# Threshold attention and a squared-ReLU network on one core: one order of steps for all periods, a weight chunk converted every second period

## The chip, the core and the metric

The kernel runs on one core of a Trainium2 chip. The metric is the device time of one launch, in microseconds, as the median of three runs. Five engines work side by side, each through its own queue in order, and wait for each other by semaphores: TensorE (PE; PEld is its weight load), VectorE (DVE), ScalarE (ACT), GpSimd (POOL) and SyncE (SP), which here issues nearly all DMAs.

## What is computed

```python
# q, k, v: (8, 8, 576, 64) float32; tau = 0.02
scores = (1 / 8) * q @ k.transpose(0, 1, 3, 2)
thresh = max(scores, axis=-1) - tau
scores = where(scores >= thresh, scores, -1e9) - max(scores)
attn = exp(scores); attn = attn / (attn.sum(-1) + 1e-9)
x = (attn @ v), heads side by side          # (4608, 512)
h = maximum(x @ w_in, 0)                    # w_in (512, 2048)
out = h * h @ w_out                         # w_out (2048, 512)
```

The two weight matrices come as 64-bit floats and are turned into 32-bit ones on the chip, by integer operations on their two halves.

## The kernel before

**Two stages.** The first is the attention, the second the network in fast-multiplication form (products of sums of blocks, seven instead of eight, twice nested). While the attention runs, the weights are fetched, converted and summed for the second stage. Nothing of the network's products starts before the attention's last products, since both need the same PSUM banks.

**Units and periods.** A unit is 128 query rows with two heads side by side. There are 144 units, two to a period (A and B), so 72 periods. For each unit the kernel makes these steps:

- `SA`, `RA`, `SB`, `RB`: scores by TensorE into six PSUM banks (L459), 512 keys and the last 64.
- `top` (L477, VectorE, two a unit): copies scores to SBUF and takes the row maximum on the way (the scores are negated, so it is a minimum). These are the maximum passes. `least` (L484, GpSimd, one a unit, 128x2) adds tau.
- `pow` (L487, ScalarE, two a unit): the exponential. `mask` (L492, VectorE, two a unit): zeroes what is under the threshold and sums. `over` and `inv` (L499 GpSimd, L502 VectorE): the reciprocal of the sums.
- `V`, `W`, `U` (L403, TensorE): turn the weights by transposes, `V` and `U` into the one pair of banks `pt`, `W` into banks 2 and 3. `Q` (L542) spreads the reciprocals beside `W`. `eV`, `eU`, `eW` (L552, ScalarE) copy them out. `T` and `eT` turn queries and keys of a later pair of heads (L423, L428, L436) in eight periods of nine.
- `PV` (L561, TensorE): the weights times the values, into the first columns of banks 0 and 5. `x` (L708 ScalarE, L710 VectorE) copies the two halves out, `xm` (L720, GpSimd) multiplies with the reciprocal, and the result goes to DRAM.

**Conversion.** A chunk of weights is 128x512 and takes six steps: `c1` (L209, ScalarE), `c2` (L216) and `c3` (L223) on GpSimd, `c4` (L231) and `c5` (L239) on VectorE, `c6` (L249) on GpSimd. There are 32 chunks. They are begun in periods 2 to 33, one in each (L592), and end one period later. Raw chunks lie in seven buffers in the part of the weight store that the block sums with outer index 5 and 3 fill later (L142, L189).

**Block sums.** 44 additions of 128x512 by GpSimd (L123, L126, made by `sums`, L261) turn the converted blocks into the operands of the network. They run after the conversion, at the steps `s1` and `s2`, and then the first operand of the network (`prepare_x`, L860) is made in the same places.

**The order.** No scheduler decides: the program's order on each engine is the order of the words in a list, one list for a period with conversion (`CONVERTING`, periods 2 to 34), one for a period without (`PLAIN`). A minus sign after a word means the step of the period before, two mean two before. Two first periods and the last ones have lists of their own. `step` (L763) makes a step once, after the same step of the earlier period. PSUM dependences between engines go by whole banks (`touch`, L378): whoever writes a bank waits for the last reader on each other engine, and a reader waits for the other engines' last access too.

The difference between the two lists that matters most is the second half of `x`: while weights are converted, ScalarE copies both halves and GpSimd scales both (L720, 128x256). Without conversion VectorE takes the second half out of PSUM and scales it at once (L710), and GpSimd scales one (128x128).

Of the kernel before, what the change touches and what calls it, by code (L numbers as in the profile page):

```python
# [48 lines left out]
def kernel(  # L49
# [54 lines left out]
    sb, cv = Region(arena, 0, X_AT[0]), Region(arena, X_AT[0], ARENA)  # L104
# [37 lines left out]
    raw_places = Region(wall, OUTER.index(5) * 7 * BANK, 49 * BANK)  # L142
# [61 lines left out]
    def convert1(m):  # L204
        if m not in raws:
            return
        lo, hi = pick(raws[m], 0), pick(raws[m], 1)
        a = cv.tile([P, WC], I32, tag="a", bufs=6, name="a")
        nc.scalar.activation(out=a.bitcast(FP32), in_=hi.bitcast(FP32), func=AF.Abs)  # L209
        parts[m] = (lo, hi, a)  # L210
        raws.pop(m)
# [49 lines left out]
    def sums(W, which, at):  # L261

        first = [at[a][b] for a in range(2) for b in range(2)]

        def inner(m, kinds):
            for op, o, x, y in kinds:
                to = W[m, o] if o == y else weight_tile(W, m, o)
                yield op(nc.gpsimd, to[:, :], W[m, x][:, :], W[m, y][:, :])

        early = which[0:3]  # L270
        for m in (1, 2):
            yield from inner(m, early)
        for op, o, x, y in which:
            for k_ in first:
                to = W[o, k_] if o == y else weight_tile(W, o, k_)
                yield op(nc.gpsimd, to[:, :], W[x, k_][:, :], W[y, k_][:, :])
        for m in OUTER:
            yield from inner(m, which[3:] if m in (1, 2) else which)
# [185 lines left out]
    def softmax(n):  # L464
# [39 lines left out]
        soft[n] = dict(top=top, least=least, power=power, mask=mask, over=over, inverse=inverse)  # L504
# [49 lines left out]
    def values(m):  # L554

        for c in range(CH):
# [35 lines left out]
    starts = {m + 2: m for m in range(16 + EARLY)}  # L592
    X_FIRST = 40
    summing = deque([sums(W_IN, SUMS_A, AT_A)])

    def sums_due(p):

        return p > max(starts) + 2 and not converts(p)

    def sums_step():  # L600
        while summing and next(summing[0], 0) == 0:
            summing.popleft()
# [10 lines left out]
    def converts(p):  # L613
        return is_wide and (has_chunk(p) or has_chunk(p - 1))

# [3 lines left out]
    def begun(n):  # L619
# [12 lines left out]
    """.split()  # L632
# [3 lines left out]
        fetch SA RA RB SB topA0 T topA1 leastA topB0 topB1 leastB powA0 powA1 eT more powB0 powB1 maskA0  # L636
        maskA1 maskB0 maskB1
        """.split(),
        1: """
        fetch ahead SA RA RB SB T eT more over topA0 topA1 leastA inv V topB0 topB1 leastB powA0 powA1 eV W  # L640
        Q powB0 eW maskA0 maskA1 powB1 maskB0 maskB1
# [3 lines left out]
    BEGIN_WITH[NU // 2 + 1] = """  # L645
        give eU-- powA0-- V-- powA1-- eV-- maskA1-- PV-- powB1-- powB0-- maskA0-- U- W-- Q-- x--
        maskB1-- maskB0-- eW-- over- inv- eU- xm-- PV- x- V- eV- W- Q- eW- xm- U eU PV x xm
        """.split()

    def spots():  # L650
        return [(sc[:, ds(b * BANK + REST, (FULL + 1) * HALF)], b * BANK) for b in (1, 4)]

# [8 lines left out]
    def period(p):  # L661

        A, B_, a, b = 2 * p, 2 * p + 1, 2 * p - 2, 2 * p - 1
        m, turns = p - 2, TURNS.get(p, ())
# [16 lines left out]
        def W():  # L681
            if has(2 * m + 2):
                pt["W"] = two_banks(w_bank(m + 1))
                fill(m + 1, "W", pt["W"], w_bank(m + 1) * BANK)

        def Q():
            if has(2 * m + 2):
                spread_sums(m + 1, pt["W"], w_bank(m + 1) * BANK)
# [8 lines left out]
        def PV():  # L697
            if has(2 * m):
                values(m)

        def values_out():
            if not has(2 * m):
                return
            late["x"] = x = sb.tile([P, 2, P], FP32, tag="x", bufs=3, name="x")
            for j in range(2):
                from_ = sc[:, ds(5 * j * BANK, P)]
                if converts(p) or j == 0:
                    made = nc.scalar.copy(x[:, j, :], from_)  # L708
                else:
                    made = nc.vector.tensor_tensor(  # L710
                        out=x[:, j, :], in0=from_, in1=wT[m][:, ts(SCALE_AT + j, P)], op=ALU.mult
                    )
                touch("x", made, 5 * j * BANK, P, m)

        def given_out():
            if has(2 * m):
                x = late.pop("x")
                made = x[:, 0 : 1 + converts(p), :].rearrange("p j n -> p (j n)")
                scale = wT[m][:, ds(SCALE_AT * P, (1 + converts(p)) * P)]
                nc.gpsimd.tensor_tensor(out=made, in0=made, in1=scale, op=ALU.mult)  # L720
                wT.pop(m)
                valued(m)
                give_x(m, x)

# [9 lines left out]
        def every(key):  # L734
# [4 lines left out]
            "U": lambda: fills("U", m), "V": lambda: fills("V", m + 1), "W": W, "Q": Q, "T": turn_some,  # L739
            "eU": lambda: evict("U", m), "eV": lambda: evict("V", m + 1), "eW": lambda: evict("W", m + 1),  # L740
            "eT": lambda: every("turn"),
            "SA": lambda: scored(A), "SB": lambda: scored(B_),
            "RA": lambda: scored_rest(A), "RB": lambda: scored_rest(B_),
            "PV": PV, "x": values_out, "xm": given_out,
            "c1": lambda: convert1(begun(p)), "c2": lambda: convert2(begun(p)),
            "c3": lambda: convert3(begun(p)), "c4": lambda: convert4(begun(p - 1)),
            "c5": lambda: convert5(begun(p - 1)), "c6": lambda: convert6(begun(p - 1)),
            "s1": lambda: sums_due(p) and sums_step(), "s2": lambda: sums_due(p) and p < 60 and sums_step(), "ahead": lambda: ahead(5), "more": lambda: ahead(7),
            "fetch": lambda: (fetch(begun(p + 2)), fetch(begun(p + 3)) if p > 1 else None), "put": put, "give": lambda: ask(False),
        }  # L750
        steps["over"] = lambda: do(a, "over")
        steps["inv"] = lambda: do(a, "inverse")
        for letter, n in (("A", A), ("B", B_)):
            for what, name in (("least", "least"),):
                steps[what + letter] = lambda n=n, name=name: do(n, name)
            for what, name in (("top", "top"), ("pow", "power"), ("mask", "mask")):
# [3 lines left out]

    tables, made_steps = {}, set()

    def step(name, p):  # L763
# [3 lines left out]
        step(name, p - 1)  # L767
        made_steps.add((name, p))
# [4 lines left out]
    def run_period(p):  # L773

        for name in BEGIN_WITH.get(p) or (CONVERTING if converts(p) else PLAIN):
# [404 lines left out]
    with tc.manual_schedule():  # L1180
        with ExitStack() as stack:
# [25 lines left out]
            for p in range(FIRST_PERIOD, NU // 2 + 6):  # L1207
# [5 lines left out]
                if p == X_FIRST + 4:  # L1213
                    summing.append(prepare_x(0, lambda op, out, x, y: op(nc.gpsimd, out, x, y)))
            for _ in range(60):
                sums_step()
# [201 lines left out]
```

## Time and profile before

| what | value |
|---|---|
| time, median of 3 runs | 1272.29 us (1269.83 to 1273.04) |
| profiled execution: its span, first to last instruction | 1273.4 us |
| what lies around the span | not shown; the span stands 1.1 us above the median of the runs |
| attention, from the first row of the trace to the network's first product | 494.8 us |
| network | 778.6 us |
| busy share of the span: PE, DVE, ACT, POOL | 98%, 78%, 66%, 77% |

The page gives the busy time of each engine over the whole span. The two stages have different limits, so the page's shares say little about the attention: its stretches have to be asked for by themselves. A view by windows gives each engine's busy time in a stretch, a timeline gives start and length of each instruction. In a full queue the distance from one start to the next is what an instruction costs; its length overlaps the next one a little (a maximum pass is 0.75 us long and the next begins 0.68 us after it).

### The profile page before, as it was taken

The numbers are of one execution on the slowest core, as the hardware profiler recorded it, in microseconds if no ns is written. First come the engines' busy times: TensorE is split into PE (matmuls) and PEld (weight loads), VectorE is DVE, ScalarE is ACT, GpSimd is POOL, SyncE is SP. The second block draws the span as 40 slices with busy tenths as digits, with TensorE's granted clock in tenths as the row PEclk, the third lists the DMA queues.
The fourth block names the chain that finished last, engine by engine and source line by source line (L and its number), as shares of the span: only waits on it lengthen the run. The fifth ranks groups of instructions, "written<-read, shape, count | busy, mean of one in ns | idle before, by whom it ended". The sixth has DMA issues, their size and how long they took to land.

```text
span 1273.4 us, 55161 instructions
## 1 busy us (share of the span) xinstructions
PE 1251.7 (98%) x22991; PEld 1093.6 (86%) x22991; DVE 988.2 (78%) x2385; ACT 844.3 (66%) x1536; POOL 982.5 (77%) x1070
## 2 busy tenths in 40 slices
PE   8999999999999999999999999999999999999998
PEld 5777776777777778988888888999999999999998
DVE  6999998999999996886887878867746654665463
ACT  6999998999999994666765856675524432443240
POOL 2999998877776542988898989868787878787776
PEclk8999999999999999999999999999999999999999
DMA  7566677434333323657667657579965336533511
GB/s 186 143 161 154 167 198 188 120 89 107 89 81 89 83 53 97 192 166 237 202 191 231 215 169 249 172 274 369 267 163 152 83 107 163 146 84 107 167 35 35
DMA packets 289912, 196.79 MB, mean 155 GB/s; under 512 B 98560, under 2 KB 250624, under 8 KB 289664
## 3 DMA queue, kind: packets, MB, share of 16 engines
q1 hardware_dynamic: 288352, 192.86, 52.8%
q8 instruction: 181, 2.97, 1.0%
q14 instruction: 67, 0.55, 0.1%
q10 hardware_dynamic: 1312, 0.41, 0.1%
HBM read 120.85 MB, written 72.35 MB: 152 GB/s over the span
## 4 chain that ended last, share of the span: by engine, by line
PE 72%; DMA 3%; ACT 2%; POOL 2%; DVE 1%; issue 1%; DVEq 0%; ACTq 0%; POOLq 0%; SPq 0%
PE po L818 27%; PE ph L997 17%; PE ph L818 10%; PE sc L561 7%; PE sc L459 6%; PE pt L403 4%; PE sc L542 1%; PE sc L423 1%; POOL arena L126 1%; DMA g<-arena 1%; ACT arena L970 1%; DVE arena L126 1%; DMA w<-arena 1%; ACT arena L971 1%; ACT c L857 1%
## 5 line engine op out<-in xcount | busy, mean ns | idle before, releaser
L126 POOL TENSOR_TENSOR arena<-arena 128x512 f32<-128x512 f32 (+1 forms) x314 | 378.7, 1224 | 125.1 <-DVE arena L126 113.5
L818 PE MATMUL po<-wall,arena 128*64 128x128 f32 x7056 | 385.8, 273 | 1.4 <-ACT arena L813 0.8
L818 PEld LDWEIGHTS po<-wall,arena 128*64 128x64 f32 x7056 | 385.1, 137 | 1.9 <-ACT arena L813 1.0
L126 DVE TENSOR_TENSOR arena<-ph,arena 128x512 f32<-128x512 f32 x378 | 254.5, 688 | 77.4 <-PE ph L997 30.9
L123 POOL TENSOR_TENSOR arena<-arena 128x128 f32<-128x128 f32 (+1 forms) x322 | 265.5, 826 | 24.1 <-DMA arena<-w 8.5
L997 PE MATMUL ph<-arena,wall 128*128 128x256 f32 x1176 | 256.7, 380 | 2.3 <-DVE arena L126 2.1
L997 PEld LDWEIGHTS ph<-arena,wall 128*128 128x128 f32 x1176 | 222.4, 190 | 36.3 <-DVE arena L126 6.2
L126 DVE TENSOR_TENSOR arena<-po,arena 128x128 f32<-128x128 f32 x378 | 107.6, 288 | 159.3 <-PE po L818 151.4
L492 DVE SCALAR_TENSOR_TENSOR arena<-arena 128x576 f32<-128x576 f32 x288 | 225.9, 820 | 0.4 <-ACT arena L487 0.3
L487 ACT ACTIVATE arena<-arena 128x576 f32<-128x576 f32 x288 | 214.1, 781 | 13.4 <-DVE arena L477 13.3
L477 DVE TENSOR_SCALAR_CACHE_REDUCE arena<-sc 128x576 f32<-128x576 f32 x288 | 203.4, 752 | 18.5 <-ACT arena L552 5.7
L857 ACT COPY c<-arena 128x512 f32<-128x512 f32 (+1 forms) x295 | 168.9, 578 | 70.1 <-DVE arena L123 36.1
L459 PE MATMUL sc<-arena 64*64 64x512 f32 (+1 forms) x2304 | 179.6, 415 | 5.6 <-ACT arena L552 1.2
L561 PE MATMUL sc<-arena 64*64 64x128 f32 (+1 forms) x5760 | 165.6, 261 | 1.0 <-ACT arena L552 0.5
L123 DVE TENSOR_TENSOR arena<-arena,c 128x512 f32<-128x512 f32 x235 | 154.2, 664 | 12.1 <-ACT c L857 7.1
L561 PEld LDWEIGHTS sc<-arena 64*64 64x64 f32 x5760 | 150.4, 133 | 4.5 <-ACT arena L552 0.7
L552 ACT COPY arena<-pt 128x1024 f32<-128x1024 f32 x143 | 145.0, 1014 | 4.6 <-PE pt L403 3.9
L459 PEld LDWEIGHTS sc<-arena 64*64 64x64 f32 x2304 | 76.8, 134 | 71.4 <-issue 47.2
L813 ACT COPY arena<-po 128x128 f32<-128x128 f32 x63 | 16.6, 264 | 177.6 <-PE po L818 174.8
L818 PE MATMUL ph<-arena,wall 128*64 128x128 f32 x2352 | 129.2, 273 | 0.6 <-DVE arena L710 0.6
L818 PEld LDWEIGHTS ph<-arena,wall 128*64 128x64 f32 x2352 | 128.3, 137 | 1.4 <-issue 1.0
L484 POOL TENSOR_SCALAR arena<-arena,tau_p 128x2 f32<-128x2 f32 x144 | 83.8, 582 | 58.5 <-DVE arena L477 44.7
(55 smaller groups left out, 1142.5 us busy)
## 6 DMA issues: line engine op xcount, KB each, us to landing
gp<-arena SPq DMA_DIRECT2D x96, 256.0 KB, 3.4
arena<-gp SPq DMA_DIRECT2D x96, 256.0 KB, 5.4
w<-arena SPq DMA_DIRECT2D x60, 256.0 KB, 2.7
wall<-w SPq DMA_DIRECT2D x49, 256.0 KB, 5.3
g<-arena SPq DMA_DIRECT2D x48, 256.0 KB, 3.7
arena<-g SPq DMA_DIRECT2D x48, 256.0 KB, 5.0
arena<-w SPq DMA_DIRECT2D x44, 256.0 KB, 3.4
arena<-in_v_dram SPq DMA_DIRECT2D x32, 288.0 KB, 3.8
```

The source lines that it names most:

```text
L123: e.tensor_tensor(out=out, in0=x, in1=y, op=ALU.subtract)
L126: e.tensor_tensor(out=out, in0=x, in1=y, op=ALU.add)
L459: made = nc.tensor.matmul(sc[at, ds(to, count)], lhs, kT[rows, ds(at_k, count)], start=True, stop=True)
L477: made = nc.vector.tensor_scalar(out=s[:, j, :], in0=sc[:, ds(at, S)], scalar1=1.0, scalar2=None, op0=ALU.mult, op1=ALU.min, accum_out=nmx ...
L484: nc.gpsimd.tensor_scalar(out=thr, in0=nmx, scalar1=tau_p[:, :], scalar2=None, op0=ALU.add)
L487: nc.scalar.activation(out=w[:, :, j, :], in_=of(j), func=AF.Exp, bias=nmx[:, j : j + 1], scale=-1.0)
L492: nc.vector.scalar_tensor_tensor(out=w[:, :, j, :], in0=of(j), scalar=thr[:, j : j + 1], in1=w[:, :, j, :], op0=ALU.is_le, op1=ALU.mult, a ...
L552: touch(kind, copy_by(joined(to), whole(pt, 0, count)), at, 2 * BANK, m)
L561: made = nc.tensor.matmul(sc[ds(u * D, D), ds(5 * j * BANK + row, count)], loaded_v[i][rows, (c - (u != j)) % CH, :], wT[m][rows, ds(weigh ...
L818: nc.tensor.matmul(to[cols], lhs[:, cols], rhs, start=start, stop=stop, skip_group_check=True)
L857: nc.scalar.copy(c, y)
L997: nc.tensor.matmul(to[:, 2 * j : 2 * j + 2, :], W_IN[m, k][:, ts(2 * h + j, P)], part_x(steps, k, m), start=(not more and j == 0), stop=Tr ...
```

## The change

One list, `PERIOD`, replaces the two. It reaches three and four periods back, and `step` now makes missing predecessors first (`NEEDS`). Every word stands for its own unit pair: `V--` is the `V` of two periods before. (`top`, `least`, `pow`, `mask` are now `t`, `l`, `p`, `m`.)

- A chunk is begun in every second period (2, 4, ... 64). `c1`, `c3`, `c2`, `c4` stand in an even period, `c5` in the next even one, `c6` in the odd one after (three periods after its begin).
- `PV` is made in two pieces (`PV` five of nine chunks of keys, `P2` the other four), and ScalarE copies out both halves of `x` in all periods but the last two (70 and 71), in which VectorE does both and scales them.
- The block sums are in three parts. The first (6 additions) may start in period 20, the second (27) in period 36, one or two in each even period; the third (11) and two thirds of the network's first operand come after period 66. `s1----` stands right after `c6---` and ahead of `lA-`, `s2` after `c2`, both on GpSimd.
- Raw chunks lie in four buffers at the end of the weight store, so that sums can be written while chunks still come; the conversion's working buffers are five instead of six and begin later in the store of the network's operand.
- The last periods get a list of their own that starts one period earlier, and results of the last four periods are sent at once.

```diff
-    sb, cv = Region(arena, 0, X_AT[0]), Region(arena, X_AT[0], ARENA)
+    sb, cv = Region(arena, 0, X_AT[0]), Region(arena, X_AT[0] + 7 * BANK, ARENA)
-    raw_places = Region(wall, OUTER.index(5) * 7 * BANK, 49 * BANK)
+    raw_places = Region(wall, 41 * BANK, 49 * BANK)
-        raw = raw_places.tile([P, 2 * WC], I32, tag="raw", bufs=7, name="raw")
+        raw = raw_places.tile([P, 2 * WC], I32, tag="raw", bufs=4, name="raw")
-        a = cv.tile([P, WC], I32, tag="a", bufs=6, name="a")
+        a = cv.tile([P, WC], I32, tag="a", bufs=5, name="a")
...
+        five, six, three, seven = which
+        def early():
+            for m in (1, 2):
+                yield from inner(m, (five, six, three))
+        def middle():
+            yield from outer((five, six, seven))
+            yield from inner(1, (seven,))
+            yield from inner(6, (five, six, three))
+            for m in (7, 4):
+                yield from inner(m, which)
+            yield from inner(5, (five, six, seven))
+        def late():
+            yield from outer((three,))
+            for m in (2, 6):
+                yield from inner(m, (seven,))
+            yield from inner(5, (three,))
+            yield from inner(3, which)
+        return early(), middle(), late()
...
-    starts = {m + 2: m for m in range(16 + EARLY)}
+    starts = {2 * m + 2: m for m in range(16 + EARLY)}
+    summing = deque([(2 * 7 + 2 + 4, early), (2 * 15 + 2 + 4, middle)])
...
-    PLAIN = """
-        put give fetch ahead eU-- powA0-- V-- powA1-- eV-- maskA1-- PV-- powB1-- c1- RA- powB0-- T--
-        maskA0-- U- W-- Q-- x-- c4- maskB1-- SA- eT-- RB- maskB0-- topA0- over- topA1- c2 s2 leastA- eW--
-        SB- topB0- s1- c5 c6 topB1- inv- leastB- xm-- c3
-    CONVERTING = """
-        put give fetch ahead SB- c1 RA topB0- powA1- c2- topB1- PV- c5- powA0- maskA0- eT- leastB- over- V-
-        x- T powB0- SA RB W- maskA1- c3 c4 inv- Q- c6- topA0 eV- topA1 leastA U xm- maskB0- powB1- eW- eU
-        maskB1- s1 s2
+    PERIOD = """
+        put give fetch ahead c6--- c1 s1---- inv-- PV--- c5-- lA- eU--- P2--- xm---- V-- pA0- tB0- c3 pA1- pB0- tB1- lB- T pB1-
+        mA1- mA0- W-- c2 RA x1--- s2 RB mB1- x0--- eV-- mB0- eT Q-- SA tA0 over- tA1 U-- c4 eW-- SB s3
+    paced = range(0, LAST_START + 4, 2)
...
+        def scaled_here(j):
+            return p >= NU // 2 - 2
...
+            "s1": lambda: p in paced and sums_step(p), "s2": lambda: p in paced and p > 35 and sums_step(p),
+            "s3": lambda: p > LAST_START + 2 and (sums_step(p), sums_step(p)),
+            "fetch": lambda: [fetch(begun(p + i)) for i in ((2, 3, 4) if p > 1 else (2,))], "put": put, "give": lambda: ask(False),
...
+    NEEDS = {
+        "V": "mA0 mA1 mB0 mB1", "U": "eV", "W": "V", "over": "mA0 mA1 mB0 mB1", "inv": "over", "Q": "W inv",
+        "eV": "V", "eU": "U", "eW": "W Q", "PV": "eV eW", "P2": "PV eU", "x0": "P2", "x1": "P2", "xm": "x0 x1",
+        "eT": "T", "c2": "c1", "c3": "c1", "c4": "c3", "c5": "c4", "c6": "c5 c2",
+    }
...
-                    summing.append(prepare_x(0, lambda op, out, x, y: op(nc.gpsimd, out, x, y)))
+                    prepare = prepare_x(0, lambda op, out, x, y: op(nc.gpsimd, out, x, y))
+                    summing.append((X_FIRST + 6, islice(prepare, 4)))
+                    summing.extend(((LAST_START + 4, prepare), (LAST_START + 4, final_)))
```

Nothing of the arithmetic of the attention or of the network changes, and no instruction of the network stage moves.

More of the change, by code (lines that the diff above doesn't have):

```diff
@@ L268, in inner, with outer @@
                 yield op(nc.gpsimd, to[:, :], W[m, x][:, :], W[m, y][:, :])
[L270 to L278, printed above, removed]
+        def outer(kinds):
+            for op, o, x, y in kinds:
+                for k_ in first:
+                    to = W[o, k_] if o == y else weight_tile(W, o, k_)
+                    yield op(nc.gpsimd, to[:, :], W[x, k_][:, :], W[y, k_][:, :])
+        five, six, three, seven = which
[16 more added lines that the diff above has]
+        return early(), middle(), late()
     later = deque()
@@ L502, in inverse @@
             nc.vector.reciprocal(out=small[:, 3, :], in_=small[:, 2, :])
-        soft[n] = dict(top=top, least=least, power=power, mask=mask, over=over, inverse=inverse)
+        soft[n] = dict(
+            top=top, least=least, power=power, mask=mask, over=over, inverse=inverse
+        )
     def do(n, what, *args):
@@ L552, in filled, with values @@
         touch(kind, copy_by(joined(to), whole(pt, 0, count)), at, 2 * BANK, m)
-    def values(m):
-        for c in range(CH):
+    def values(m, cs):
+        for c in cs:
             for u in range(2):
@@ L590, in has, with sums_step @@
         return 0 <= n < NU
-    starts = {m + 2: m for m in range(16 + EARLY)}
+    starts = {2 * m + 2: m for m in range(16 + EARLY)}
     X_FIRST = 40
[L594 to L601, printed above, removed]
+    LAST_START = max(starts)
+    early, middle, final_ = sums(W_IN, SUMS_A, AT_A)
+    summing = deque([(2 * 7 + 2 + 4, early), (2 * 15 + 2 + 4, middle)])
+    def sums_step(p):
+        while summing and p >= summing[0][0]:
+            if next(summing[0][1], 0) != 0:
+                return
             summing.popleft()
@@ new lines, in period @@
+            "s3": lambda: p > LAST_START + 2 and (sums_step(p), sums_step(p)),
+            "ahead": lambda: ahead(5), "more": lambda: ahead(7),
+            "fetch": lambda: [fetch(begun(p + i)) for i in ((2, 3, 4) if p > 1 else (2,))], "put": put, "give": lambda: ask(False),
+            "over": lambda: do(A, "over"), "inv": lambda: do(A, "inverse"),
+        }
+        for f in "VU":
+            steps[f] = lambda f=f: fills(f, m)
+        for f in "VUW":
+            steps["e" + f] = lambda f=f: evict(f, m)
@@ L753, in period @@
         for letter, n in (("A", A), ("B", B_)):
-            for what, name in (("least", "least"),):
-                steps[what + letter] = lambda n=n, name=name: do(n, name)
-            for what, name in (("top", "top"), ("pow", "power"), ("mask", "mask")):
+            steps["l" + letter] = lambda n=n: do(n, "least")
+            for what, name in (("t", "top"), ("p", "power"), ("m", "mask")):
                 for j in range(2):
@@ L767, in step @@
         step(name, p - 1)
+        for other in NEEDS.get(name, "").split():
+            step(other, p)
         made_steps.add((name, p))
```

98 lines of the change are left out of this document (49 added, 49 removed).

## The prediction

> **What bounds the kernel now.** First the page, for the span; then the busy time by stretches; then timelines of single periods.
>
> ```profile
> span 1273.4 us, 55161 instructions
> ```
> ```profile
> 99.00:201.15 102.15, 99.66 (x2566) 74.49 (x2568) 101.62 (x287) 100.55 (x184) 94.87 (x106) 1.00 0.67 175
> 259.70:450.90 191.20, 190.87 (x5180) 143.47 (x5176) 183.58 (x541) 180.21 (x309) 132.00 (x174) 1.00 0.40 91
> 1000.00:1200.00 200.00, 200.00 (x3670) 200.00 (x3668) 117.44 (x307) 71.77 (x148) 156.13 (x132) 1.00 0.46 134
> ```
>
> Columns: length, then busy time of PE, PEld, DVE, ACT, POOL, the granted clock, DMA. The third row is the network: PE is full, and the change moves nothing there, so that stage only starts earlier or later. The first row is attention with conversion: VectorE is busy 101.6 of 102.2 us and ScalarE 100.6, so neither has room. The second is attention without: PE leads, the others have a few per cent. The maximum passes alone, in the same stretches, give the length of a period (eight records each, with the reading of the accumulator):
>
> ```profile
> 99.00:201.15 102.15, 43.11 (x120) 1.00 0.67 175
> 259.70:450.90 191.20, 84.03 (x240) 1.00 0.40 91
> ```
>
> So 15 periods took 102.15 us, **6.81 us** each with conversion, and 30 took 191.2, **6.37 us** without. Where the costs lie is read from starts. VectorE and ScalarE in one period with conversion:
>
> ```profile
> 136.46 0.75 DVE L477 TENSOR_SCALAR_CACHE_REDUCE arena<-sc 128x576 f32<-128x576 f32 x1
> ...
> 137.14 0.69 DVE L239 SCALAR_TENSOR_TENSOR wall<-wall,arena 128x512 int32<-128x512 int32 x1
> 137.74 0.81 DVE L492 SCALAR_TENSOR_TENSOR arena<-arena 128x576 f32<-128x576 f32 x1
> ...
> 138.48 0.81 DVE L492 SCALAR_TENSOR_TENSOR arena<-arena 128x576 f32<-128x576 f32 x1
> ...
> 139.22 0.44 DVE L231 TENSOR_SCALAR arena<-arena 128x512 int32<-128x512 int32 x1
> 139.58 0.16 DVE L502 RECIPROCAL arena<-arena 128x4 f32<-128x4 f32 x1
> ```
> ```profile
> 134.23 1.01 ACT L552 COPY arena<-pt 128x1024 f32<-128x1024 f32 x1
> 135.14 0.70 ACT L209 ACTIVATE arena<-wall 128x512 f32<-128x512 f32 x1
> 135.74 1.42 ACT L487 ACTIVATE arena<-arena 128x576 f32<-128x576 f32 x2
> 137.07 0.67 ACT L436 COPY arena<-sc 128x256 f32<-128x256 f32 x2
> 137.64 0.32 ACT L428 ACTIVATE arena<-sc,qscale 128x64 f32<-128x64 f32 x1
> 137.85 0.43 ACT L708 COPY arena<-sc 128x128 f32<-128x128 f32 x2
> 138.15 0.81 ACT L487 ACTIVATE arena<-arena 128x576 f32<-128x576 f32 x1
> ```
> ```profile
> 277.91 0.58 ACT L552 COPY arena<-sc 128x512 f32<-128x512 f32 x1
> 278.39 1.02 ACT L552 COPY arena<-pt 128x1024 f32<-128x1024 f32 x1
> ```
>
> (The third fence is a period without conversion; the first leaves out the records of 0.08 us that read the accumulator.) Start to start: a maximum pass 0.68, c5 0.60, a mask 0.74, c4 0.36; the reciprocal is 0.16 long; a large copy 0.91, c1 0.60, an exponential 0.67, the turned keys 0.57 + 0.21, one half of x 0.15, the small copy 0.48. In a period with conversion VectorE needs 4 x 0.68 + 4 x 0.74 + 0.16 + 0.36 + 0.60 = 6.80 of 6.81 us, and ScalarE 4 x 0.67 + 2 x 0.91 + 0.48 + 0.78 + 0.30 + 0.60 = 6.66. Both are full. Without conversion VectorE needs 5.84 and its half of x, ScalarE 5.91, and PE at most the whole period, 6.37.
>
> **The change part by part.**
>
> *The mix of periods.* The even periods of the new list carry what a converting period carries now, on VectorE and ScalarE to the instruction: 6.80 and 6.66. An odd one has no conversion on either, and the second half of x on ScalarE: VectorE 5.84, ScalarE 6.06. If every period stood for itself, even ones would take 6.81, odd ones PE's 6.37, a pair 13.18, and that is what one period of each kind takes today: the change would give nothing. What can be won is that a full even period leans on a slack odd one. The floor of a pair is then the fullest engine: ScalarE 12.72, VectorE 12.64, PE at most 12.74. I take **12.96 per pair, the middle of 12.74 and 13.18**, because the leaning can only be partial: PV overwrites the banks that the last maximum pass has read, so a VectorE that is late in an even period makes PE late at once, and ScalarE's copies after it. For more than nothing speaks that c4, the reciprocal and c5 stand at the seam of two periods, between the last maximum pass of A and the first of B, where VectorE has to wait for SB in any case.
>
> In periods 2 to 66 the kernel now has 33 x 6.81 + 32 x 6.37 = 428.6 us; the new one 32.5 pairs, 421.2. **Term: -7.4 us**, bounds -14.5 (12.74) and -0.2 (13.18); both ends are kept.
>
> *GpSimd.* It must do in one pair what the rows give:
>
> ```profile
> 274.06 0.29 POOL L484 TENSOR_SCALAR arena<-arena,tau_p 128x2 f32<-128x2 f32 x1 [0.18 <-DVE arena L477]
> 274.32 1.27 POOL L126 TENSOR_TENSOR wall<-wall 128x512 f32<-128x512 f32 x1
> 275.57 0.79 POOL L484 TENSOR_SCALAR arena<-arena,tau_p 128x2 f32<-128x2 f32 x1
> ```
> ```profile
> L216 POOL TENSOR_SCALAR wall<-wall 128x512 int32<-128x512 uint32 x32 | 52.5, 1640 | 2.7
> ...
> L720 POOL TENSOR_TENSOR arena<-arena 128x256 f32<-128x256 f32 x33 | 39.8, 1205 | 0.0
> ...
> L499 POOL TENSOR_SCALAR arena<-arena 128x4 f32<-128x4 f32 x72 | 29.1, 404 | 60.8 <-DVE arena L492 58.7
> L223 POOL TENSOR_SCALAR arena<-arena 128x512 f32<-128x512 f32 x32 | 21.3, 665 | 4.7 <-ACT arena L209 2.2
> L249 POOL TENSOR_TENSOR arena<-wall 128x512 int32<-128x512 int32 x16 | 16.6, 1038 | 0.2
> ```
>
> A `least` takes 0.29 beside a maximum pass and 0.79 where a mask stands beside it: GpSimd waits for the mask's end. From period 36 a pair has two additions (2.54), c2, c3, c6 (3.34), two xm (2.41), four `least` (1.16 to 3.16) and two `over` (0.80): 10.3 to 12.3 us of 12.96; without the second addition, before period 36, 1.27 less. (A mean of one stands behind the bar, in ns.) It is hidden, but `lA` now stands behind an addition or c6, and both masks of unit A behind `lA`; if that cover goes, masks come late by what it is over. I cost it at nothing, bounds 0 and +10 (the third rival below). The additions' own places gain little, since they stand beside maximum passes today too; a mask that starts under an addition's last 0.27 us,
>
> ```profile
> 275.32 0.88 DVE L492 SCALAR_TENSOR_TENSOR arena<-arena 128x576 f32<-128x576 f32 x1
> ```
>
> took 0.88 instead of 0.81, 0.07 more; 44 additions make 3 us of that at most, in periods where VectorE is not the first bound: nothing taken.
>
> By the Trainium skill (SBUF — State Buffer, Who interferes with whom) a VectorE instruction with two SBUF inputs and a GpSimd instruction that reads SBUF exclude each other for the whole instruction, whoever starts first. The row of 275.32 agrees. By that rule c2, which the new order puts beside masks, would block them; the row of c2 below speaks against it.
>
> ```profile
> 136.53 1.64 POOL L216 TENSOR_SCALAR wall<-wall 128x512 int32<-128x512 uint32 x1
> ```
>
> It runs to 138.17, the mask of 137.74 stands under its last 0.43 us and takes 0.81 like the next one. By that row c2 blocks no mask, and moving it under masks costs nothing; the other way is the fourth rival.
>
> *The other buffers and queues.* A raw chunk is held from its fetch, four periods ahead of its begin, to c6, three after: seven periods at two a chunk, 3.5 of four buffers. SP's fetch waits for a c6 that stands one period earlier; behind it in SP's queue are loads of queries and keys wanted periods later. Half as many fetches per period. Nothing, bounds 0 and +2.
>
> *The ends.* Periods 67 to 71 have no conversion before or after, and PE led there: nothing. After the last scores PE has the same products left as now; VectorE takes both halves of the last two pairs: +0.7 (bounds -0.5, +2). The third part of the sums, 11 additions, 14 us, now stands after the last `over`:
>
> ```profile
> 488.48 0.23 POOL L499 TENSOR_SCALAR arena<-arena 128x4 f32<-128x4 f32 x1 [1.54 <-DVE arena L492]
> ...
> 505.41 1.28 POOL L126 TENSOR_TENSOR arena<-arena 128x512 f32<-128x512 f32 x1 [10.38 <-DVE arena L126]
> ```
>
> From 488.7 to 505.4 GpSimd has 16.7 us with only three short products in it (two of which go to VectorE), so the 14 us end at about 503, ahead of the network's first need of GpSimd. Nothing; without the cover, up to +2.
>
> **Sum**: -7.4 + 0.7 = -6.7. Against the span of 1273.4 that is 1266.7. The page gives no time of its own run beside the span; the median of the runs stands 1.1 lower, which would be 1265.6. I say **1266**. One stall of this execution has nothing to do with the change and may be absent next time:
>
> ```profile
> 208.00:210.00 2.00, 2.00 (x19) 0.98 (x22) 0.02 (x1) 1.69 (x2) 1.41 (x2) 0.70 0.87 270
> ```
>
> At a granted clock of 0.70 VectorE, otherwise full, is busy 0.02 of 2 us. It is in the range, not in the sum.
>
> **The rivals.**
>
> 1. *Full leaning*: pairs at the floor, 12.74: -14.5 + 0.7, 1259. For: the seam. Against: three engines would have to stay within 1% of each other without a wait, and today's period without conversion stands 0.46 above ScalarE's need.
> 2. *No leaning*: the change does in effect not what it says, pairs 13.18: 1273. For: the same instructions stand in the even period. Against: its queues are reordered over three periods.
> 3. *GpSimd becomes the bound* from period 36. If each of the two additions also waits for a mask (0.74), the pair needs 12.3 + 1.5 = 13.8; `lA` then comes late and with it VectorE and all after. 16 pairs x (13.8 - 13.18) = +10, no gain in the pairs before, +0.7 at the end: **1283**. It decides from the point where GpSimd's pair is over 13.18. For: 12.3 is near. Against: two of four `least` stand beside maximum passes.
> 4. *c2 blocks masks after all*: in each even period one mask waits out what is left of a c2 of 1.64 us, say all but one mask's 0.74: 32 x 0.90 = +29: 1302. For: the addition that held up the mask of 275.32. Against: the c2 of 136.53. This is the Trainium skill's rule of exclusion from above, taken whole.
>
> **How the numbers follow.** Chances: the forecast 0.42, full leaning 0.13, no leaning 0.17, GpSimd 0.25, c2 0.03. About 0.3%, 4 us, is what a measurement of this kernel can tell from no change. Faster: 0.37 of the forecast's 0.42, all of the first rival, 0.03 of the second: 0.53. Slower: the last two and 0.03: 0.31. The same: 0.16. The likeliest case alone spans 1260 to 1271; 1256 to 1282 takes in the others and leaves out half of the third rival, the fourth, and the far side of the first: 2 in 10.
>
> **What would show it.** Maximum passes counted over periods 4 to 66 give the pair: 12.96 right, 13.18 or more wrong. Alternate periods should differ by less than 0.4 us, where leaning works. VectorE idle before the first mask of a period, released by L504's `least` on GpSimd, shows the third rival; masks well over 0.81 beside L217 the fourth; idle time of PE before the network's first product much over half a microsecond, or of its second block, would show that the late sums are not hidden. The step most open to error is the 12.96, taken between two ends.

## The result, and the profile after

The changed kernel takes **1274.8 us** (median of 19 runs, 1272.62 to 1280.67), the kernel before 1269.83 on the same chip (19 runs); the ratio is 1.0042, 95% interval 1.0031 to 1.0053. It is slower by 0.4%, some 5 us, where 6.7 us less were forecast.

The profiled execution of before has the longer span of the two (1273.4 us against 1271.0), although its kernel is the quicker one: it holds the stall that the prediction set aside. So the period is compared, not the span. The first two rows are the maximum passes of before, from the start of period 2 to that of period 66, and in the 17 us around the stall; then the same stretch of after. (Columns: the stretch, its length, busy time and count, granted clock, DMA.)

```profile
22.74:450.96 428.22, 181.81 (x512) 0.99 0.53 130
205.13:222.06 16.93, 5.77 (x17) 0.90 0.69 188
222.06:235.56 13.50, 5.76 (x17) 1.00 0.46 118
```
```profile
21.35:450.85 429.50, 183.22 (x512) 1.00 0.52 133
35.40:246.62 211.22, 91.56 (x256) 1.00 0.51 126
246.62:450.85 204.23, 85.93 (x240) 1.00 0.52 135
```

The pair with the stall took 16.93 us, the next pair 13.50: without it before has 428.22 - 3.4 = 424.8, and after 429.5, **4.7 us more** in the same 64 periods. The last two rows cut after at period 36, where the second addition of a pair begins: 16 pairs at 211.22 / 16 = **13.20** and 15 at 204.23 / 15 = **13.62** (middle values 13.1 and 13.65; the means hold a few longer pairs). The forecast was 12.96 for both. VectorE has become full in the second stretch too, as the busy times of all engines show there (order as before: PE, PEld, DVE, ACT, POOL):

```profile
101.80:207.40 105.60, 103.33 (x2774) 74.78 (x2766) 103.74 (x289) 102.70 (x189) 70.20 (x92) 1.00 0.50 124
255.70:438.60 182.90, 176.91 (x4610) 124.81 (x4603) 181.39 (x485) 173.63 (x317) 148.28 (x176) 1.00 0.53 137
```

VectorE is busy 181.4 of 182.9 us in the second row (a mask that is held up counts as busy), where by the prediction's distances from start to start its instructions need 13.5 pairs x 12.64 = 170.6. What grew is the length of the masks, as the page's groups say (busy time, mean ns of one, idle before them); in before the same 288 masks took 225.9 us, 820 ns each.

```profile
L512 DVE SCALAR_TENSOR_TENSOR arena<-arena 128x576 f32<-128x576 f32 x288 | 239.5, 884 | 0.7 <-POOL arena L504 0.3
```

13.6 us more, and next to no waiting for `least` (L504): 0.3 us over the whole run. Two kinds of mask are long. The first, in every second period; GpSimd, then VectorE (start, length):

```profile
138.15 0.79 POOL L504 TENSOR_SCALAR arena<-arena,tau_p 128x2 f32<-128x2 f32 x1
139.03 1.97 POOL L217 TENSOR_SCALAR wall<-wall 128x512 int32<-128x512 uint32 x1
```
```profile
138.71 0.82 DVE L512 SCALAR_TENSOR_TENSOR arena<-arena 128x576 f32<-128x576 f32 x1
...
139.46 1.20 DVE L512 SCALAR_TENSOR_TENSOR arena<-arena 128x576 f32<-128x576 f32 x1
...
140.59 0.81 DVE L512 SCALAR_TENSOR_TENSOR arena<-arena 128x576 f32<-128x576 f32 x1
```

c2 (L217) is issued under the mask of 138.71 and waits for its end, about 139.4. Then it goes first, and the mask of 139.46 takes 1.20 us, 0.40 more. The next mask, which stands under the rest of c2, takes 0.81. This is so with all 31 c2's that stand beside masks (0.37 to 0.48 more, in the mean 0.42).

The second kind appears from period 36. GpSimd, from the second addition (409.34) to `xm` (L737), and the first mask after it:

```profile
409.34 1.47 POOL L124 TENSOR_TENSOR wall<-wall 128x512 f32<-128x512 f32 x1
410.90 0.52 POOL L519 TENSOR_SCALAR arena<-arena 128x4 f32<-128x4 f32 x1
411.50 1.04 POOL L250 TENSOR_TENSOR arena<-wall 128x512 int32<-128x512 int32 x1
412.52 0.29 POOL L504 TENSOR_SCALAR arena<-arena,tau_p 128x2 f32<-128x2 f32 x1
412.78 0.73 POOL L737 TENSOR_TENSOR arena<-arena 128x256 f32<-128x256 f32 x1
```
```profile
412.91 1.21 DVE L512 SCALAR_TENSOR_TENSOR arena<-arena 128x576 f32<-128x576 f32 x1
```

The addition ends at 410.81, when the first two of the four maximum passes beside which `over`, c6, `lA` and `xm` should stand are nearly through. GpSimd has no gap from there to `xm`, which is still running when the first mask comes. In periods 36 to 66 an `xm` holds a mask 14 times, by 0.10 to 0.40, 4.9 us in all.

The ends are nearly as forecast. The network begins 10.8 us after the start of the last maximum pass (before 10.4), and the late additions are done before GpSimd is wanted again:

```profile
490.01 8.66 POOL L124 TENSOR_TENSOR wall<-wall 128x512 f32<-128x512 f32 x7
498.61 1.29 POOL L127 TENSOR_TENSOR wall<-wall 128x512 f32<-128x512 f32 x1
499.98 3.85 POOL L124 TENSOR_TENSOR wall<-wall 128x512 f32<-128x512 f32 x3
506.16 1.27 POOL L127 TENSOR_TENSOR arena<-arena 128x512 f32<-128x512 f32 x1 [2.33 <-DVE arena L127]
```

### The profile page after: what moved, and what is told of

Read it like the earlier page. It is cut to its first block, busy times and chain, and to the rows that moved or that the text cites. A ratio compares the mean times of both kernels' runs of the same rounds, so it can differ in the third digit from the quotient of the medians.

```text
span 1271.0 us, 55038 instructions
## 1 busy us (share of the span) xinstructions
PE 1248.7 (98%) x22991; PEld 1077.4 (85%) x22991; DVE 1000.3 (79%) x2350; ACT 848.7 (67%) x1571; POOL 972.9 (77%) x1068
## 4 chain that ended last, share of the span: by engine, by line
PE 76%; ACT 9%; DVE 7%; issue 3%; POOL 3%; DMA 2%; SPq 0%; ACTq 0%; POOLq 0%; DVEq 0%
PE po L852 30%; PE ph L1031 15%; PE ph L852 9%; PE sc L583 8%; PE sc L479 7%; PE pt L423 4%; DVE arena L497 4%; ACT arena L574 3%; ACT arena L507 3%; DVE arena L512 2%; POOL arena L127 1%; PE sc L443 1%; PE sc L564 1%; ACT arena L448 1%; ACT arena L1005 1%
## 5 line engine op out<-in xcount | busy, mean ns | idle before, releaser
L512 DVE SCALAR_TENSOR_TENSOR arena<-arena 128x576 f32<-128x576 f32 x288 | 239.5, 884 | 0.7 <-POOL arena L504 0.3
L507 ACT ACTIVATE arena<-arena 128x576 f32<-128x576 f32 x288 | 205.7, 785 | 11.4 <-DVE arena L497 10.5
L583 PEld LDWEIGHTS sc<-arena 64*64 64x64 f32 x5760 | 161.0, 133 | 56.0 <-DVE arena L497 40.6
L479 PE MATMUL sc<-arena 64*64 64x512 f32 (+1 forms) x2304 | 189.5, 419 | 5.4 <-ACT arena L574 3.8
L583 PE MATMUL sc<-arena 64*64 64x128 f32 (+1 forms) x5760 | 177.4, 262 | 5.9 <-DVE arena L497 4.3
L574 ACT COPY arena<-pt 128x1024 f32<-128x1024 f32 x143 | 146.9, 1028 | 14.3 <-PE pt L423 12.7
L423 PEld LDWEIGHTS pt<-ident,arena 64*128 64x128 f32 x2288 | 82.3, 139 | 69.9 <-ACT arena L574 32.5
L504 POOL TENSOR_SCALAR arena<-arena,tau_p 128x2 f32<-128x2 f32 x144 | 94.0, 653 | 46.8 <-DVE arena L497 26.1
```

The costliest lines, as they stand in the source:

```text
L423: made = nc.tensor.transpose(pt[:, r, ts(slot, HALF)], of[rows, :], ident[rows, rows])
L479: made = nc.tensor.matmul(sc[at, ds(to, count)], lhs, kT[rows, ds(at_k, count)], start=True, stop=True)
L507: nc.scalar.activation(out=w[:, :, j, :], in_=of(j), func=AF.Exp, bias=nmx[:, j : j + 1], scale=-1.0)
L512: nc.vector.scalar_tensor_tensor(out=w[:, :, j, :], in0=of(j), scalar=thr[:, j : j + 1], in1=w[:, :, j, :], op0=ALU.is_le, op1=ALU.mult, a ...
L574: touch(kind, copy_by(joined(to), whole(pt, 0, count)), at, 2 * BANK, m)
L583: made = nc.tensor.matmul(sc[ds(u * D, D), ds(5 * j * BANK + row, count)], loaded_v[i][rows, (c - (u != j)) % CH, :], wT[m][rows, ds(weigh ...
```

## The experiments

All start from the changed kernel; each time stands beside runs of the kernel before on the same chip (medians 1269.7 to 1270.7). The ratios are to these, and where two runs come from different chips the difference of their ratios is the safer measure. The theory: the pair of 12.96 is lost to two things, a mask held by each c2 (first and second half), and the second addition, which pushes GpSimd's later work under masks (second half).

**The second addition left out.** A DMA fills its tile, so the network's weights are wrong.

```diff
-                yield op(nc.gpsimd, to[:, :], W[m, x][:, :], W[m, y][:, :])
+                yield filler(to) if muted else op(nc.gpsimd, to[:, :], W[m, x][:, :], W[m, y][:, :])
...
-            "s2": lambda: p in paced and p > 35 and sums_step(p),
+            "s2": lambda: p in paced and p > 35 and unmade(p),
```

> The changed kernel without the additions of step s2 (14 of the 44 block sums are left out; their places are filled by a DMA instead, so the network's weights are wrong). Theory (in periods 36 to 66 the second addition makes GpSimd late, c6, lA and xm move back, and xm then stands beside a mask and holds it up by 0.40): masks of 1.2 us beside xm go from 17 to nearly none, a pair falls from 13.6 to the 13.1 of the first half, the whole by 6 to 9 us. Rival (GpSimd's lateness is hidden, the second half is longer for another reason): the pair stays over 13.4, the whole falls by less than 3.

Measured: 1270.64 us, ratio 1.0002 [0.9991, 1.0012]. Periods 4 to 36, then 36 to 66:

```profile
39.35:250.61 211.26, 91.54 (x256) 1.00 0.51 125
250.61:450.09 199.48, 85.82 (x240) 1.00 0.59 155
```

The first stretch is unchanged, 13.20; the second is 13.30 instead of 13.62 (middle value 13.11 instead of 13.65). GpSimd and the first mask behind its `xm` (L748) in such a pair:

```profile
409.64 0.23 POOL L525 TENSOR_SCALAR arena<-arena 128x4 f32<-128x4 f32 x1 [0.52 <-DVE arena L518]
409.95 1.04 POOL L250 TENSOR_TENSOR arena<-wall 128x512 int32<-128x512 int32 x1
...
411.40 0.73 POOL L748 TENSOR_TENSOR arena<-arena 128x256 f32<-128x256 f32 x1
```
```profile
412.61 0.81 DVE L518 SCALAR_TENSOR_TENSOR arena<-arena 128x576 f32<-128x576 f32 x1
```

`over` now waits for the masks (0.52), `xm` has ended at 412.13, and the first mask takes 0.81; one `xm` alone still holds a mask in these periods, where 14 did. The 14 additions cost 4.2 us between the two medians, 5.1 by the ratios, 4.8 between the two windows, about what the holds by `xm` had added up to. The pair is as expected, the whole fell short of the 6 to 9 us.

**c2 left out.** c6 adds zeros in its place (the low half of each weight is missing).

```diff
-        nc.gpsimd.tensor_tensor(out=a, in0=hi, in1=lo, op=ALU.add)
+        nc.gpsimd.tensor_tensor(out=a, in0=hi, in1=lo if isinstance(m, tuple) else zeros.bitcast(I32), op=ALU.add)
...
-            "c1": lambda: convert1(begun(p)), "c2": lambda: convert2(begun(p)),
+            "c1": lambda: convert1(begun(p)), "c2": lambda: None,
```

> The changed kernel without c2 in the attention (32 of 32; c6 adds zeros in place of the low halves, so the weights lose their last bits). Theory: the 31 masks of 1.2 us beside c2 are 0.81, pairs fall by 0.40 to 12.7 in the first half and by 0.4 to 0.6 in the second, the whole by 12 to 17 us. Rival (hand-offs): pairs fall by less than 0.1, the whole by less than 3.

Measured: 1275.76 us, 1.0045 [1.0028, 1.0062], no better in all: missed.

```profile
37.57:245.58 208.01, 91.53 (x256) 1.00 0.52 126
245.58:453.98 208.40, 85.62 (x240) 1.00 0.51 132
```

In the first half a pair falls by 0.20, to 13.00 (middle value 12.94): the held mask was worth 0.40 on VectorE, but no more than half of it shows in the pair. In the second half it rises to 13.89. There the second addition has moved to c2's place:

```profile
395.35 1.75 POOL L126 TENSOR_TENSOR wall<-wall 128x512 f32<-128x512 f32 x1
```
```profile
395.15 0.81 DVE L514 SCALAR_TENSOR_TENSOR arena<-arena 128x576 f32<-128x576 f32 x1
...
395.89 1.83 DVE L514 SCALAR_TENSOR_TENSOR arena<-arena 128x576 f32<-128x576 f32 x1
```

An addition that is issued under a mask holds the next one for 1.02 us, not 0.40: until 0.19 us before its own end. So leaving c2 out isn't a clean test where an addition follows it, and the next run takes both away.

**Both left out.**

> Both left out: c2 (c6 then adds zeros: wrong weights) and the second addition of each pair (a DMA fills its tile). If the held mask of c2 and the second addition are all that lies between the forecast's 12.96 and what was measured, pairs are 12.90 to 13.00 throughout, periods 4 to 66, and the time is 1264 to 1267, the forecast. Rival: something third costs in the second half (DMA, more prepared work): pairs of 13.1 or more there, and 1268 to 1271.

Measured: **1265.33 us**, 0.9964 [0.9950, 0.9978].

```profile
36.36:244.01 207.65, 91.59 (x256) 1.00 0.52 126
244.01:441.12 197.11, 85.82 (x240) 1.00 0.60 158
```
```profile
L520 DVE SCALAR_TENSOR_TENSOR arena<-arena 128x576 f32<-128x576 f32 x288 | 222.5, 825 | 0.6 <-POOL arena L512 0.5
```

12.98 and 13.14 a pair, middle values 12.94 and 12.90; the mask is back at 825 ns. The middle values are the forecast's pair. The second mean is not: it holds three long pairs. In two of them (13.92 and 13.90) an addition for the network's operand, which this run still makes at the step `s2`, holds a mask for 1.00 us; this is the "more prepared work" of the rival. In the third (14.27) PE stands still for 1.1 us at 345.7, and the profile shows nothing that it waited for. The other twelve pairs have 12.92.

**c3 twice.** c3 (clamping a second time changes nothing) stands ahead of c2 too, beside masks.

```diff
-        mA1- mA0- W-- c2 RA x1--- s2 RB
+        mA1- mA0- W-- c3b c2 RA x1--- s2 RB
```

> The changed kernel with c3 (clamp, the same result when made twice) made a second time right ahead of c2, among the masks. It adds 0.61 us of GpSimd in 32 periods. Theory (a GpSimd instruction that reads SBUF holds up the mask that it meets, and VectorE has no slack): one more mask of each even period is held up by 0.2 to 0.4, the whole rises by 6 to 13 us. Rival (only the length of GpSimd's own queue counts): rises by 0 to 3.

Measured: 1292.21 us, 1.0177 [1.0162, 1.0192], 17 us more: the right sign, but more than expected.

```profile
37.00:254.59 217.59, 91.44 (x256) 1.00 0.50 121
254.59:468.28 213.69, 86.13 (x240) 1.00 0.50 129
```
```profile
142.47 1.08 POOL L224 TENSOR_SCALAR arena<-arena 128x512 f32<-128x512 f32 x1
143.64 1.97 POOL L217 TENSOR_SCALAR wall<-wall 128x512 int32<-128x512 uint32 x1
```
```profile
143.01 1.15 DVE L512 SCALAR_TENSOR_TENSOR arena<-arena 128x576 f32<-128x576 f32 x1
...
144.10 1.20 DVE L512 SCALAR_TENSOR_TENSOR arena<-arena 128x576 f32<-128x576 f32 x1
```

Both hold a mask, 0.34 and 0.39 us. The pair goes to 13.60 in the first stretch (0.40 more, no less than the added hold of 0.34) and to 14.25 in the second (0.63 more): where the second addition follows, everything on GpSimd also gets later.

**c2 elsewhere, first trial.** In the odd period, behind `xm`; the second addition behind `over`.

```diff
-        ... xm---- V-- ... W-- c2 RA x1--- s2 RB ... over- tA1 U-- c4
+        ... xm---- c2- V-- ... W-- RA x1--- RB ... over- s2 tA1 U-- c4
```

> The changed kernel with c2 moved on GpSimd from among the masks of the even period to right behind xm in the odd one, beside the maximum passes of B, and the second addition moved behind `over`. Theory (VectorE is full, and every c2 holds up one mask by 0.40 us: 31 masks of 1.2 us instead of 0.81): no mask stands at 1.2 beside c2 in periods 4 to 34, a pair of periods there falls from 13.1 to about 12.75, the whole by 5 to 12 us against the changed kernel (1274.8), so 1263 to 1270. Rival (the pair is set by the hand-offs between PE, ScalarE and VectorE; the held-up mask eats slack): the pair stays at 13.1 within 0.1 and the time at 1275 within 2.

Measured: 1285.54 us, 1.0121 [1.0106, 1.0136]: missed.

```profile
36.07:246.87 210.80, 91.77 (x256) 1.00 0.51 124
246.87:463.02 216.15, 85.77 (x240) 1.00 0.49 127
```
```profile
L512 DVE SCALAR_TENSOR_TENSOR arena<-arena 128x576 f32<-128x576 f32 x288 | 235.7, 864 | 15.1 <-POOL arena L504 14.6
```

The first half gains next to nothing, although c2 now starts ahead of the masks and the held mask takes only 0.08 to 0.13 more there:

```profile
131.61 1.65 POOL L217 TENSOR_SCALAR wall<-wall 128x512 int32<-128x512 uint32 x1
```
```profile
132.00 0.91 DVE L512 SCALAR_TENSOR_TENSOR arena<-arena 128x576 f32<-128x576 f32 x1
```

The middle pair falls from 13.11 to 13.03, where leaving c2 out gave 12.94. So three quarters of the hold are gone, and only half of its effect; what takes up the other half in this order isn't shown. In the second (14.41 a pair) the addition ahead of c6 makes `least` late, and VectorE waits 14.6 us for it; c2 holds its mask for 0.40 again. This is what the third rival described, but it needed another order.

**c2 elsewhere, second trial.** In the even period, right behind c1, where GpSimd was idle beside two maximum passes; for the chunks of periods 2 to 16 alone, so that one half of the run stays as a control.

```diff
-        put give fetch ahead c6--- c1 s1----
+        put give fetch ahead c6--- c1 c2e s1----
...
-            "c2": lambda: convert2(begun(p)),
+            "c2": lambda: p < 18 or convert2(begun(p)), "c2e": lambda: p > 17 or convert2(begun(p)),
```

> For the chunks begun before period 18, c2 stands right behind c1, where GpSimd is idle beside two maximum passes; later chunks as after. Theory (a c2 that has been running for 0.4 us holds no mask, one that starts under a mask holds the next one for 0.4 us): in periods 4 to 18 no mask beside c2 takes over 0.9 us, and the pairs go from 13.1 to about 12.95, as with c2 left out, unless c3 is pushed under a mask instead (then 13.05). Rival: c2 holds a mask wherever it stands: 13.1 with masks at 1.2. Total 1 us less at most; pairs in periods 20 to 66 unchanged (13.10 and 13.65).

Measured: 1272.42 us, 1.0016 [1.0002, 1.0031]. First after, then this kernel, in periods 4 to 18:

```profile
35.40:128.29 92.89, 40.08 (x112) 1.00 0.53 130
```
```profile
36.55:127.56 91.01, 40.24 (x112) 1.00 0.53 126
```
```profile
95.03 1.62 POOL L217 TENSOR_SCALAR wall<-wall 128x512 int32<-128x512 uint32 x1
```

Seven pairs at 13.00 instead of 13.27; the run without c2 has 12.92 there, so three quarters of what leaving c2 out gives comes from its place alone. In the pair shown c2 ends at 96.65, ahead of the masks, and the first of them, at 98.12, takes 0.82. Of the 31 masks that c2 held 25 are left in the run. c2 costs what the place where it begins makes it cost. The time fell by 2.4 us where 1 at most was expected; the windows give 1.9 in the moved stretch, the rest is within the scatter of the runs.

**Which engine sets the pair.** The second half of `x` is given back to VectorE in odd periods.

```diff
-            return p >= NU // 2 - 2
+            return p >= NU // 2 - 2 or (j == 1 and p % 2 == 0)
```

> The second half of x (128x128) is copied by VectorE in odd periods too, as in the kernel before; xm then adds 128x128 there. VectorE gets about 0.2 us more per pair, ScalarE 0.2 us less, GpSimd half an xm less in those periods. If VectorE sets the pair, pairs in periods 4 to 36 go from 13.10 to 13.2 to 13.3 and the time from 1274.8 to 1277 to 1281. Rival: ScalarE sets it: pairs fall to about 12.95 and the time to 1271 to 1273.

Measured: 1277.6 us, 1.0061 [1.0041, 1.0081], 2.8 us more. The middle pair in periods 4 to 36 goes from 13.11 to 13.27, as expected if VectorE sets the pair. Relieving ScalarE gains nothing; VectorE sets the pair, though not alone (33 times 0.2 us were added, and less than half of it shows).

**The second addition on VectorE**, in the odd period behind its masks.

```diff
-        ... x1--- s2 RB ... mB0- eT Q-- SA tA0
+        ... x1--- RB ... mB0- s2- eT Q-- SA tA0
...
-                yield op(nc.gpsimd, to[:, :], W[m, x][:, :], W[m, y][:, :])
+                yield op(adder(), to[:, :], W[m, x][:, :], W[m, y][:, :])
```

> The second addition of each pair, from period 36, is done by VectorE in the odd period (one addition of about 0.7 us more on VectorE, 1.3 us less on GpSimd). If GpSimd's lateness costs 0.55 a pair and VectorE is full to within 0.2 us, the pair in periods 36 to 66 is 13.1 + 0.7 - 0.2 = 13.6, and the time stays at 1273 to 1276. Rival: VectorE has more room in odd periods (about 0.7 us by its work): 13.1 to 13.3, and 1268 to 1271, a version as quick as the kernel before.

Measured: 1273.22 us, 1.0020 [1.0006, 1.0034], mean and middle value of a pair 13.53 and 13.45 from period 36. This is near the 13.6 of the theory: VectorE has no 0.7 us to spare in odd periods.

**The mends together.** c2 early where it gains, ten second additions on VectorE, four of the late ones on VectorE at the end.

```diff
+    early_c2 = (*range(0, 20), 32, 34)
...
-            "s2": lambda: p in paced and p > 35 and sums_step(p),
+            "s2": lambda: p in paced and 35 < p < 56 and sums_on_vector(p),
```

> What the runs so far point to, in one kernel: c2 right behind c1 for the chunks of periods 2 to 18, 32 and 34 (where no addition stands in that place); the second additions on VectorE in odd periods, and only up to period 54 (10 instead of 14); four of the late additions on VectorE ahead of the network's first evictions, so that GpSimd's late work stays at about 13.5 us. By the sizes measured: 11 pairs at 0.27 less, 10 pairs at 0.2 less, 4 to 5 pairs at 13.1 instead of 13.65: 7 to 8 us less than the changed kernel's 1274.8, up to 0.5 more at the end: 1267 to 1268, 0.1 to 0.25% under the kernel before. Rival: the costs don't add (what c2 no longer holds, c3 and xm hold in its place; VectorE's additions cost as much as GpSimd's did): 1270 to 1273, no better than the kernel before.

Measured: 1273.09 us, 1.0028 [1.0018, 1.0038]: missed. Periods 4 to 18, 30 to 34, 36 to 66, 66 to 71 (after has 31.76 in the last):

```profile
36.24:126.40 90.16, 40.19 (x112) 1.00 0.53 128
...
205.66:233.53 27.87, 11.45 (x32) 1.00 0.41 98
...
246.58:447.12 200.54, 85.67 (x240) 1.00 0.53 137
447.12:481.18 34.06, 14.29 (x40) 1.00 0.16 38
```
```profile
453.61 1.28 POOL L127 TENSOR_TENSOR wall<-wall 128x512 f32<-128x512 f32 x1
454.96 2.51 POOL L124 TENSOR_TENSOR wall<-wall 128x512 f32<-128x512 f32 x2
```

The first and third stretch gain as expected (12.88 and 13.37 a pair). In periods 30 to 34 c2 met an addition in the same place (13.9 a pair), and one of the last periods got three additions in a row (second fence): 4 us given back in two places.

**The same without these two collisions** (`early_c2` is 0 to 22, 36 and 38; no addition in the step of period 64).

> As mended, but c2 stands early only in periods where no addition stands in the same place (2 to 22, 36, 38: in mended it met one in periods 32 and 34, pairs 13.9), and period 68 has two additions instead of three. By the rows of mended: 1.7 us back at periods 30 to 34, some 1 us more from four more early c2's, 1.3 us in period 67: 1273.1 - 4 = about 1269, within 0.1% of the kernel before. Rival: other waits take the place of these: 1271 to 1273.

Measured: 1270.35 us, 0.9997 [0.9988, 1.0006]: level with the kernel before, 0.45% under the changed kernel by the ratios.

**The early c2 with all second additions on VectorE.**

> The early c2 of mended_spread with all second additions on VectorE (as in second_sum_on_vector), and the last periods as in the changed kernel. 1273.2 less 12 to 13 pairs at 0.27: 1269.5 to 1270.5, level with the kernel before. Rival as before: 1271 to 1273.

Measured: 1271.29 us, 1.0008 [0.9999, 1.0018], a microsecond more than expected. No version tried that makes all of the weights beats the kernel before.

## Why the prediction was wrong

*What bounds it, the pair of 12.96.* With the two costs below away the middle values of a pair are 12.94 and 12.90. But 12.96 was the middle of two ends, not worked out, and no run says why the pair lands there: that it came so near is luck in part. The kernel does lean: with both costs away alternate periods take 6.38 and 6.58 in the second half, and pairs of 12.7 occur, near the floor of 12.74. In the changed kernel they take 6.67 and 7.00. The mean of all pairs without the two costs is higher than the middle value, and the term of -7.4 comes to -5.3:

```profile
21.58:441.12 419.54, 183.18 (x512) 1.00 0.57 144
```

The kernel before took 424.8 for the same 64 periods; in the changed kernel the term came to +4.7. That the run took 1265.3 us where 1266 was forecast is luck too: the forecast stood on a median of three runs, 1272.29, and 19 runs gave 1269.83, 2.5 us less. From there -6.7 would have been 1263.

*"c2 blocks no mask, and moving it under masks costs nothing."* This step failed, and with it the chance of 0.03 for the fourth rival was far too small, though its price was far too high. The row it rested on was true: a mask that comes 1.2 us after the start of c2 isn't held. But it showed c2 that had begun beside a maximum pass, and the change lets it begin under a mask. Then it is the next mask that waits, for some 0.40 us only. Price: 31 masks at about 0.40, some 13 us of VectorE, of which about 5 us show in the time (5.3 from 1270.64 to 1265.33, 4.8 by the ratios); by the second trial with c2 elsewhere about three quarters of that is its place, and the rest its being there at all. The sign that the prediction had named for this rival, masks well over 0.81 beside L217, is what the trace shows. By the Trainium skill (SBUF — State Buffer, Who interferes with whom) the port is held for the whole instruction: the addition of 395.35 agrees to within 0.19 us, and so does the row of 275.32 in the prediction, whose mask took 0.07 more and not 0.27; c2 doesn't, since the mask of 139.46 ended its waiting 1.14 us ahead of c2's end.

*"GpSimd: I cost it at nothing, bounds 0 and +10."* The value failed, the bounds held: 4.2 us (1274.8 to 1270.64), 5.1 by the ratios. The sum of busy time, 10.3 to 12.3 of 12.96, said that there was room. There was none where it was needed: the masks stand in a row of four, and beside them the instructions of GpSimd that the runs show either wait or hold a mask. That leaves the stretch beside the maximum passes, and `over`, c6 or an addition, `lA` and `xm` fill it. The third rival had the right place and nearly the right pair (13.8 for 13.65), and the wrong way: `lA` was hardly ever late (0.3 us), but what stands behind it, `xm`, came under the first mask.

*The additions' own places, the buffers and queues, the ends.* The additions' first places cost next to nothing (middle pairs of 13.1 with them in periods 20 to 30, 13.04 in the two pairs behind these, without). ScalarE never sat idle ahead of c1, the first to need a raw chunk. The end cost 0.4 us for 0.7 forecast, and the late additions are hidden. Periods 66 to 71, costed at nothing, took 31.76 us instead of 31.32: `xm` is 128x256 there now and holds masks too, five of them by 0.40 to 0.47 up to the end of the attention.

*The chances.* Both costs had been named, and 0.42 went to a case with neither. Nor do they stand apart: the addition follows c2 in GpSimd's queue, so where c2 is away the addition takes its place.

## What to carry to other kernels

A price read from one row holds for the place in which that row stood: ask under what an instruction would begin, not only beside what it would run. When busy time of an engine is summed up against a period, count only those stretches in which it may work without holding another engine. And test two suspected costs together as well as one by one: leaving out c2 alone showed no gain, because the addition moved into its place.

## What the runs showed of the hardware

- Three kinds of GpSimd instruction that read SBUF hold a mask (VectorE, two inputs in SBUF) until 0.19 to 0.20 us before their own end: 16 additions of 128x512 in the run without c2, 19 `xm` of 128x256 in after, 31 of the added c3 of 128x512. c2, a multiplication of 32-bit integers of the same size, lets go 1.13 to 1.16 us before its end, 31 of 31 times in after; the mask then takes some 0.40 more.
- It goes the other way too: c2 issued under a mask is 1.97 us long, 1.62 beside maximum passes; `least` 0.79 and 0.29. The maximum passes, which read PSUM, are 0.72 to 0.77 long beside all of them, 288 of 288 in after.
- VectorE's work and its time are not the same: 31 waits of about 0.40 us (some 13 us) were worth about 5 us of the kernel. In the same stretches ScalarE and PE are busy to about 95% or more (102.7 and 103.3 of 105.6 us, 173.6 and 176.9 of 182.9), which may be why; no run separates it.
